# Two decode attentions in one kernel: PE's loop takes in the last chunk, and the fill products at a chunk's head get a count by chunk

## The chip, the cores and the metric

The kernel runs on one core of a Trainium2 chip. A core has a matrix engine (PE), a vector engine (DVE), a scalar engine (ACT), a general engine (POOL), a sync engine (SP) that here only issues transfers, and 16 DMA engines that move data between the device's memory (HBM) and the core's two memories, SBUF and, for PE's results, PSUM. The metric is the device time of one execution in microseconds (us). The span in a profile goes from the first to the last instruction; the time of the same execution is a little longer.

## The reference

Two attentions for one new token each, side by side, both with batch 4, 32 query heads of 128 and a cache of 8192 positions in bf16. A has 8 key heads, each shared by four query heads, and looks at the last W = 2048 positions; B has 32 key heads and looks at all.

```python
def _A_ref(x, k_cache, v_cache, wq, wo):
    q = (x @ wq).reshape(B, 1, 32, 128).transpose(0, 2, 1, 3)
    k = jnp.repeat(k_cache[:, :, Sk - W:, :], 4, axis=1)
    v = jnp.repeat(v_cache[:, :, Sk - W:, :], 4, axis=1)
    p = softmax(einsum("bhqd,bhkd->bhqk", q, k) * 128 ** -0.5)
    o = einsum("bhqk,bhkd->bhqd", p, v)
    return o.transpose(0, 2, 1, 3).reshape(B, 1, 4096) @ wo      # B x 1 x 512

# _B_ref: the same over the whole cache, with a key head for each query head
return jnp.concatenate([a, b], axis=-1)                         # 4 x 1 x 1024
```

Nearly all bytes are caches: 4 x 32 x 8192 x 128 x 2 bytes x 2 = 537 MB for B, and 34 MB for A.

## The kernel before

**Chunks.** A is cut into 8 chunks (a key head with the four batches), B into 32 (four heads of one batch): 256 tiles of 128 positions of K and as many of V, 8 MB each. Chunks of B are counted here from 0 to 31 (in the code `c - NCA`). Four chunks in a row share a piece of B's wo (512 KB).

**A chunk of B on PE** (`whole_B`, L910). First `reorder` (L820) multiplies the piece of wo, which lies in `wos`, into another order in four PSUM banks (three of `tr` and `po`); DVE takes these into `wol` (`take_wol`, L830). Between the two stand the fill products, `keep_busy(NBUSY)` (L905): products 128x512 of the identity into a bank of `sc`, which nobody reads. Then 32 groups of 8 transposes of K (`emit_T`, L541) into `tr`, whose results DVE and ACT copy to `kt`, and two groups later their scores (`emit_S`, L581, into `sc`). The first three groups of transposes need `wol`'s copies, since they take the same banks. The softmax is made in two halves (row maximum, the maximum over partitions, exp on ACT into `pbb`). Then 256 products with V (`emit_pv`, L733), the first 128 into `po`, the others into a bank of `tr`; then `norm_out` (DVE, into `oz`) and `emit_fin` (L835), eight products 4x256 of `oz` with `wol` that add to the bank `fin` over all 32 chunks. The stop flag of these products is set in the last products of the last chunk alone.

**Loops.** Every engine's program is written out as a list of operations with waits; `mark` (L90) cuts it at chunks. `_Sched.runs` (L123) looks for chunks whose operations read the same and whose waits differ by constant steps, and `emit_looped` (L164) writes such a run as a loop with its waits counted by a register; the rest is written out straight. The comparison holds what an operation says, its stop flag too; so PE's loop over B covers chunks 0 to 30, and chunk 31 is straight code behind it. An operation with `at` is given the register's value, by which it finds a place that moves from chunk to chunk.

**Transfers.** SP issues all large ones, in a fixed order on one queue: K of a chunk, V of it, K of the next. K of the next chunk waits until half of this chunk's K is transposed (L406, through POOL, which moves K's second half to a spare place, L421), V of the next until the products with V are through (L445). In the last chunks K and V come in pieces. Behind B's last V come the last two pieces of A's wo (L360); the products of A's last two chunks with them stand at the end of PE's program, and then the two halves of the output are copied by DVE (`emit_out`, L856) and stored.

Of the kernel before, what the change touches and what calls it, by code (L numbers as in the profile page):

```python
# [10 lines left out]
BF16 = mybir.dt.bfloat16  # L11
F32 = mybir.dt.float32

P = 128
# [18 lines left out]
QK = (0, 4, 8)  # L33
QC = (16, 24)
QV = (0, 8, 16, 24, 28)
NBUSY = 3

TRM0, BC0, L0, Q0, XT0 = 0, 256, 288, 320, 448
Z0 = Q0
# [18 lines left out]
class _Sched:  # L58
# [61 lines left out]
    def emit(self, engname, eng, sems):  # L120
        self.emit_ops(self.ops[engname], eng, sems)
# [55 lines left out]
def bass_concat_heads__sliding_block_cached__mha_block_cached__decode_kernel(  # L177
        nc, A_x, A_k, A_v, A_wq, A_wo, B_x, B_k, B_v, B_wq, B_wo, out):
    NB = A_x.shape[0]
# [4 lines left out]
    DO = A_wo.shape[1]  # L184
# [22 lines left out]
    NC = len(chunks)  # L207
    NCA = Hkv
# [13 lines left out]
    sch = _Sched()  # L222
    with ExitStack() as es:
        block = es.enter_context(nc.Block())

        def sb(name, shape, dt):
            return es.enter_context(nc.sbuf_tensor(name, shape, dt))

        def ps(name, shape, dt):
            return es.enter_context(nc.psum_tensor(name, shape, dt))  # L230
# [10 lines left out]
        identb = sb("identb", [P, P], BF16)  # L241
# [23 lines left out]
        pbt = {0: sb("pba", [P, NPB, NTA * 16 + NW], BF16), 1: sb("pbb", [P, 2, NTB * 2 + NW], BF16)}  # L265
        oT = sb("oT", [P, NSM, 16], BF16)
        oz = sb("oz", [P, 16], BF16)
        outsb = sb("outsb", [P, DO // 2], BF16)
        sel4 = sb("sel4", [P, 4, P], BF16)
        zA = sb("zA", [P, 2, 16], BF16)  # L270
# [4 lines left out]
        sc = ps("sc", [P, 2, 512], F32)  # L275
        po = ps("po", [P, 512], F32)
        ms = ps("ms", [P, 512], F32)
        fin = ps("fin", [P, 512], F32)
# [20 lines left out]
            out=ind[:, :].rearrange("u (x i) -> u x i", x=4), in_=onesf[0:4, :].rearrange("u (x i) -> u x i", x=4),  # L299
            pattern=[[1, 4], [0, P // 4]], compare_op=ALU.is_equal, fill=0.0, base=0, channel_multiplier=-1),  # L300
            waits=["c_onesf", "c_identf"], key="c_ind")
        sch.add("pool", lambda e: e.memset(oz[:, :], 0.0), waits=["c_ind"], key="c_oz")
        sch.add("pool", lambda e: e.memset(qb[:, :, :], 0.0), waits=["c_oz"])
        sch.add("pool", lambda e: e.memset(qq[:, :], 0.0), key="c_qb")

# [46 lines left out]
        def wo_slot(g):  # L352
            return g % 2
# [137 lines left out]
        def pe_mm(o, l, r, start=True, stop=True, transpose=False, waits=(), key=None):  # L491
            if transpose:
                sch.add("pe", lambda e: e.transpose(o, l, r), waits, key)  # L493
            else:
                sch.add("pe", lambda e: e.matmul(o, l, r, start=start, stop=stop), waits, key)  # L495
# [73 lines left out]
        def emit_qb(c, spare=False):  # L569

            if c >= NCA and not spare:
                col = NB * HQ + 4 * (c - NCA)
                sch.add("act", lambda e, x=0: e.activation(qq[:, 0:4], qs[:, bass.ds(x + col, 4)], ACTF.Copy), at=col,
                        waits=["c_qb"] + ([("S", chunks[c - 1]["s_last"])] if c > NCA else []), key=("qb", c))
                return
            waits = ["c_qb", ("q", 0)] if c < 2 else [("S", chunks[c - 2]["s_last"])]
            n, col = 16, 16 * c
            sch.add("dve", lambda e, x=0: e.tensor_copy(qb[:, c % 2, 0:n], qs[:, bass.ds(x + col, n)]), at=col,
                    waits=waits + ([("q", 1)] if c == 1 else []), key=("qb", c, "spare") if spare else ("qb", c))

        def emit_S(s):  # L581
            c, g = groups[s]
            ch = chunks[c]
            for t in range(TG):
                j = g * TG + t
                if ch["ab"] == 1:
                    bank, o0 = j // (NTB // 2), 4 * (j % (NTB // 2))
                else:
                    bank, o0 = j // HT, 16 * (j % HT)

                n = min(NW, 512 - o0)
                q = qb[:, c % 2, 0:n] if ch["ab"] == 0 else qq[:, 0:n]
                waits = []
                if t == 0:
                    waits = [("ev", s)] + sc_read[bank]
                    if g == 0:
                        waits += [("qb", c)]
                    sc_read[bank] = []
                pe_mm(sc[:, bank, o0:o0 + n], kt[:, s % NKT, t * P:(t + 1) * P], q,
                      waits=waits, key=("S", s) if t == TG - 1 else None)  # L600
# [184 lines left out]
        def add_first(c):  # L785

            pe_mm(po2[:, 0:4], identf[:, :], t1[:, :], start=False, stop=False, waits=[("t1", c)], key=("add", c))
            po_read[:] = [("t1", c)]
# [28 lines left out]
        def reord_at(u):  # L817
            return po[:, :] if u == 3 else tr[:, u, :].bitcast(F32)

        def reorder(c):  # L820

            for u in range(4):
                pp = slice(u * P // 4, (u + 1) * P // 4)
                for r in range(4):
                    pe_mm(reord_at(u), back[pp, r, :], wos[pp, r, :], start=r == 0, stop=r == 3,
                          waits=[("wr", c), ("c_back", 3)] if u == r == 0 else [],
                          key=("reord", c, u) if r == 3 else None)
            po_read[:] = [("wol", c, 3)]

        def take_wol(c):  # L830
            for u in range(4):
                o = reord_at(u)
                sch.add("dve", lambda e, u=u, o=o: e.tensor_copy(wol[:, u, :], o), waits=[("reord", c, u)], key=("wol", c, u))  # L833

        def emit_fin(c):  # L835
            ab = 0 if c < NCA else 1
            if ab == 1:
                ov = oz[:, :].rearrange("p (b u) -> p b u", b=NB)
                ops = [(ov[:, :, u], wol[:, u, :]) for u in range(4)]
                waits = ["c_oz", ("oT", c)]  # L840
            else:
                w = wor[:, wo_slot(c), :].rearrange("p (r n) -> p r n", r=4)
                ops = [(zA[:, c % 2, r * NB:(r + 1) * NB], w[:, r, :]) for r in range(4)]
                waits = [("z", c), ("wo", c)]
            lastc = NC - 1 if ab == 1 else NCA - 1

            for i, (l, r) in enumerate(ops):
                for h, (p0, x) in enumerate(out_halves(ab)):
                    pe_mm(fin[p0:p0 + NB, 0:DO // 2], l, r[:, x], start=False,
                          stop=i == len(ops) - 1 and c == lastc, waits=waits if i == h == 0 else [],  # L850
                          key=("fin", c) if i == len(ops) - 1 and h == 1 else None)

        def out_halves(ab):
            return [(64 * (1 - ab) + 32 * h, slice(h * DO // 2, (h + 1) * DO // 2)) for h in (0, 1)]

        def emit_out(c):  # L856
            ab = 0 if c < NCA else 1
            at = out_halves(ab)
            rows = slice(at[0][0], at[1][0] + NB)
            sch.add("dve", lambda e: e.tensor_copy(outsb[rows, :], fin[rows, 0:DO // 2]), waits=[("fin", c)], key=("osb", ab))  # L860
            for h, (p0, x) in enumerate(at):
                sch.add_dma("sp" if h else "act", lambda e, x=x, p0=p0: e.dma_start(out[:, 0, ab * DO + x.start:ab * DO + x.stop], outsb[p0:p0 + NB, :]),
                            "d_o%d" % h, waits=[("osb", ab)], key=("out", ab, h))
# [41 lines left out]
        def keep_busy(n):  # L905

            for _ in range(n):
                pe_mm(sc[:, 1, :], identb[:, :], sel4[:, :, :].rearrange("p r x -> p (r x)"))

        def whole_B(c):  # L910


            ch = chunks[c]
            sch.mark()
            reorder(c)
            keep_busy(NBUSY)
            take_wol(c)
            emit_qb(c)
            for g in range(ch["NG"]):
                emit_T(ch["s"] + g)  # L920
                if g >= SLAG:
                    emit_S(ch["s"] + g - SLAG)
                if g == 18:
                    stats_rowmax(c, 0)
                if g == 20:
                    stats_gmax(c, 0)
                if g == 22:
                    stats_bc(c, 0)
                if g == 23:
                    exp_B(c, 0, (0, 1))  # L930
                if g == 26:
                    exp_B(c, 0, (2, 3))
            for g in range(SLAG):
                emit_S(ch["s_last"] + 1 - SLAG + g)
            stats_rowmax(c, 1)
            for g in range(ch["NG"]):
                emit_pv(c, g)
                if g == 4:
                    stats_gmax(c, 1)
                if g == 8:  # L940
                    stats_bc(c, 1)
                    sums_B(c, 0)
                    exp_B(c, 1, (0, 1, 2, 3))
                    weigh_B(c)
                    sums_B(c, 1)
                    rest_sums(c)
                if g == 24:
                    norm_sum(c)
                if g == ch["NG"] - 2:
                    add_first(c)  # L950
            norm_out(c)
            emit_fin(c)

        def finish_A():
# [19 lines left out]
        for c in range(NCA, NC):  # L974
            whole_B(c)
        sch.mark()
        for c in range(NCA - LATEWO, NCA - 1):
            emit_fin(c)
        emit_out(NC - 1)
# [61 lines left out]
```

## Time and profile before

| | us |
|---|---|
| median of three runs | 1376.79 (1372.24 to 1378.86) |
| the profiled execution | 1376.78 |
| its span | 1375.0 |
| PE busy | 1200.1 |
| DVE, ACT, POOL busy | 770.3, 520.7, 234.5 |

In the profile's lists, L495 is the helper that records PE's products and L493 the one that records transposes, so groups are told apart by the tiles that they write and read (`tr<-identb,kv` is a transpose of K, `sc<-sel,identb` a fill product, `tr<-pbb,kv` and `po<-pbb,kv` the products with V). "<-POOLq L80" is a wait for the counter by which POOL passes on that K or V has landed. A number in brackets is the engine's idle time before the row and what ended it; "issue" means that nothing the profile shows was waited for. In rows of windows come the window, its length, busy time and instructions of PE, PE's weight loads, DVE, ACT and POOL, the granted clock of PE, the busy share of DMA and its GB/s.

### The profile page before, as it was taken

What the parts mean: (1) busy time and instruction counts of PE and PEld (TensorE: products, weight loads), DVE (VectorE), ACT (ScalarE), POOL (GpSimd) and SP (SyncE); (2) the same over time, 40 slices, a digit from 0 to 9 for tenths busy, and PEclk for the clock granted to TensorE, in tenths of its full rate; (3) what the DMA queues carried; (4) which work ended last, traced back from release to release, by engine and by line L of the source; (5) the groups of instructions that cost most, each with busy time, mean ns of one, the idle gap of its engine ahead of it and who ended that gap; (6) DMA issues with size and microseconds to landing.
All of it is one profiled execution on the core that took longest, in us unless ns stands there. A gap on an engine that the chain in (4) does not pass through costs nothing.

```text
span 1375.0 us, 62434 instructions
## 1 busy us (share of the span) xinstructions
PE 1200.1 (87%) x27697; PEld 1123.1 (82%) x27697; DVE 770.3 (56%) x1559; ACT 520.7 (38%) x713; POOL 234.5 (17%) x429
## 2 busy tenths in 40 slices
PE   4788788988888998989898998989899898999997
PEld 4787788878788988878788988878798788888887
DVE  1775455656455565645565565646556565555654
ACT  1553234333333443423343443323344342443443
POOL 2000002222220222222211222222112222000000
PEclk9998999999999999999999999999999999999999
DMA  9999999999999999999999999999999999999997
GB/s 401 423 428 429 427 443 427 431 429 429 438 435 435 433 431 431 431 431 433 438 427 435 435 425 433 415 450 418 429 431 429 440 423 427 437 427 425 428 427 330
DMA packets 18077, 587.64 MB, mean 427 GB/s; under 512 B 2024, under 2 KB 2048, under 8 KB 4096
## 3 DMA queue, kind: packets, MB, share of 16 engines
q1 hardware_dynamic: 18016, 587.21, 99.4%
q8 instruction: 21, 0.34, 0.1%
q14 instruction: 8, 0.07, 0.0%
q10 hardware_dynamic: 32, 0.01, 0.0%
HBM read 587.21 MB, written 0.01 MB: 427 GB/s over the span
## 4 chain that ended last, share of the span: by engine, by line
DMA 48%; PE 44%; issue 3%; DVE 3%; ACT 2%; ACTq 0%; SPq 0%; DVEq 0%; POOLq 0%
DMA kv<-in_B_k_cache_dram 43%; PE tr L493 24%; PE sc L495 11%; PE tr L495 4%; PE po L495 3%; DMA kv<-in_B_v_cache_dram 2%; DMA kv<-in_B_wq_dram 2%; PE ms L495 1%; DMA kv<-in_A_k_cache_dram 1%; DVE kt L564 1%; DVE wol L833 1%; ACT pba L716 1%; ACT pbb L686 1%; PE fin L495 1%; DVE sA L617 0%
## 5 line engine op out<-in xcount | busy, mean ns | idle before, releaser
L493 PE MATMUL tr<-identb,kv 128*128 128x128 bf16 x8704 | 683.2, 225 | 85.2 <-POOLq L80 73.9
L564 DVE COPY kt<-tr 128x1024 bf16<-128x1024 bf16 x736 | 503.2, 691 | 290.1 <-PE tr L493 287.1
L562 ACT ACTIVATE kt<-tr 128x1024 bf16<-128x1024 bf16 x352 | 359.7, 1024 | 698.9 <-PE tr L493 696.7
L493 PEld LDWEIGHTS tr<-identb,kv 128*128 128x128 bf16 x8704 | 529.2, 101 | 103.8 <-issue 69.9
L495 PE MATMUL sc<-qq,kt 128*128 128x64 bf16 x8192 | 403.5, 193 | 15.6 <-DVE kt L564 13.3
L421 POOL COPY kv<-kv 128x512 int32<-128x512 int32 x400 | 224.6, 616 | 923.1 <-DMA kv<-in_B_k_cache_dram 923.1
L495 PEld LDWEIGHTS sc<-qq,kt 128*128 128x128 bf16 x8192 | 333.6, 99 | 24.2 <-DVE kt L564 13.5
L686 ACT ACTIVATE pbb<-sc,negb 32x128 bf16<-32x128 f32 x256 | 138.0, 539 | 137.3 <-DVE negb L668 134.5
L495 PE MATMUL tr<-pbb,kv 128*128 128x64 bf16 x4096 | 135.6, 193 | 27.4 <-ACT pbb L686 25.5
L495 PEld LDWEIGHTS tr<-pbb,kv 128*128 128x128 bf16 x4096 | 130.9, 99 | 31.2 <-issue 30.3
L495 PE MATMUL po<-pbb,kv 128*128 128x64 bf16 x4096 | 135.1, 194 | 5.5 <-issue 4.4
L495 PEld LDWEIGHTS po<-pbb,kv 128*128 128x128 bf16 x4096 | 127.5, 98 | 5.3 <-issue 3.3
L833 DVE CAST wol<-tr 128x512 bf16<-128x512 f32 x96 | 60.4, 685 | 54.3 <-PE tr L495 52.6
L693 DVE TENSOR_REDUCE rs<-pbb 128x4 f32<-128x512 bf16 x32 | 22.0, 686 | 50.3 <-ACT pbb L686 50.3
L766 DVE RECIPROCAL ib<-ms 128x8 f32<-128x8 f32 x32 | 6.7, 208 | 57.7 <-PE ms L495 57.7
L495 PE MATMUL tr<-wos,back 32*128 32x512 bf16 x384 | 34.8, 383 | 0.4 <-issue 0.4
L495 PE MATMUL po<-wos,back 32*128 32x512 bf16 x128 | 33.9, 384 | 0.0
L654 DVE TENSOR_REDUCE gm<-ms 4x4 f32<-4x128 f32 x72 | 19.8, 275 | 20.8 <-PE ms L493 20.8
L634 DVE TENSOR_REDUCE rh<-sc 128x4 f32<-128x512 f32 x32 | 22.1, 692 | 14.3 <-PE sc L495 14.3
L668 DVE TENSOR_SCALAR negb<-ms 128x4 f32<-128x4 f32 x64 | 10.1, 157 | 32.0 <-PE ms L495 32.0
L495 PE MATMUL sc<-qb,kt 128*128 128x64 bf16 (+3 forms) x512 | 25.8, 195 | 2.1 <-issue 1.6
L495 PE MATMUL sc<-sel,identb 128*128 128x512 bf16 x96 | 26.9, 390 | 0.0
(82 smaller groups left out, 459.3 us busy)
## 6 DMA issues: line engine op xcount, KB each, us to landing
kv<-in_B_k_cache_dram SPq DMA_DIRECT2D x15, 2048.0 KB, 24.9
kv<-in_B_k_cache_dram SPq DMA_DIRECT2D x6, 4096.0 KB, 19.4
kv<-in_B_v_cache_dram SPq DMA_DIRECT2D x5, 4096.0 KB, 26.2
kv<-in_B_v_cache_dram SPq DMA_DIRECT2D x9, 2048.0 KB, 27.3
kv<-in_A_k_cache_dram SPq DMA_DIRECT2D x8, 2048.0 KB, 14.1
kv<-in_A_v_cache_dram SPq DMA_DIRECT2D x8, 2048.0 KB, 15.6
kv<-in_A_wq_dram SPq DMA_DIRECT2D x1, 4096.0 KB, 12.3
kv<-in_B_wq_dram SPq DMA_DIRECT2D x1, 4096.0 KB, 27.2
```

The costliest lines, as they stand in the source:

```text
L421: sch.add("pool", lambda e, dst=dst, org=org: e.tensor_copy(dst, org), waits=[("T", s0 + ch["NG"] - 1)] if g == 0 else [])
L493: sch.add("pe", lambda e: e.transpose(o, l, r), waits, key)
L495: sch.add("pe", lambda e: e.matmul(o, l, r, start=start, stop=stop), waits, key)
L562: sch.add("act", lambda e: e.activation(dst, src, ACTF.Copy), waits=waits, key=("ev", s))
L564: sch.add("dve", lambda e: e.tensor_copy(dst, src), waits=waits, key=("ev", s))
L634: sch.add("dve", lambda e: e.tensor_reduce(out=dst, in_=src, axis=AX.X, op=ALU.max), waits=[("S", ch["s"] + (half + 1) * ch["NG"] // 2 - 1 ...
L654: sch.add("dve", lambda e: e.tensor_reduce(out=gm[0:C, m, 0:U], in_=src, axis=AX.X, op=ALU.max), waits=[key_of("trm", c, half)], key=key_o ...
L668: sch.add("dve", lambda e: e.tensor_scalar(out=negb[:, m, 0:C], in0=ms[:, col:col + C], scalar1=-scale, scalar2=None, op0=ALU.mult), waits ...
L686: sch.add("act", lambda e, src=src, dst=dst, pp=pp, u=u: e.activation(dst, src, ACTF.Exp, bias=negb[pp, half, u:u + 1], scale=scale), wait ...
L693: sch.add("dve", lambda e: e.tensor_reduce(out=dst, in_=probs_of(c, half).rearrange("p j u -> p u j"), axis=AX.X, op=ALU.add), waits=[("ex ...
L716: sch.add("act", lambda e, b=b: e.activation(probs_of(c).rearrange("p j (b c) -> p j b c", b=NB)[:, :, b, :], eA[:, c % 2, :].rearrange("p ...
L833: sch.add("dve", lambda e, u=u, o=o: e.tensor_copy(wol[:, u, :], o), waits=[("reord", c, u)], key=("wol", c, u))
```

## The change

1. The stop flag of B's fin products is the same in all chunks (off). The sum is closed instead by two products with zeros behind the loop, one for each half of `fin`; DVE's copy of B's output waits for the second. A column block of zeros `zz` is made by POOL at the start for them.
2. With that, all 32 chunks of B say the same, and PE's loop covers them all; no chunk of B is left as straight code.
3. Two plain fill products stand at a head in place of three, and behind them a loop on PE over one more: it runs once in chunks 0 to 7 and 24 to 31, and eight times (1 + MOREBUSY) in chunks 8 to 23. Its count is worked out from the register of the loop over chunks.

```diff
-NBUSY = 3
+NBUSY = 2
+MOREBUSY = 7
...
+        zz = sb("zz", [P, NB], BF16)
...
-        sch.add("pool", lambda e: e.memset(oz[:, :], 0.0), waits=["c_ind"], key="c_oz")
+        sch.add("pool", lambda e: e.memset(oz[:, :], 0.0), waits=["c_ind"])
+        sch.add("pool", lambda e: e.memset(zz[:, :], 0.0), key="c_oz")
...
-            lastc = NC - 1 if ab == 1 else NCA - 1
...
-                          stop=i == len(ops) - 1 and c == lastc, waits=waits if i == h == 0 else [],
+                          stop=i == len(ops) - 1 and c == NCA - 1, waits=waits if i == h == 0 else [],
...
-            sch.add("dve", lambda e: e.tensor_copy(outsb[rows, :], fin[rows, 0:DO // 2]), waits=[("fin", c)], key=("osb", ab))
+            sch.add("dve", lambda e: e.tensor_copy(outsb[rows, :], fin[rows, 0:DO // 2]), waits=[("end", 32) if ab else ("fin", c)], key=("osb", ab))
...
+        def more_busy(c):
+            n = c - NCA
+            def mm(e):
+                return e.matmul(sc[:, 1, :], identb[:, :], sel4[:, :, :].rearrange("p r x -> p (r x)"), start=True, stop=True)
+            def emit(e, x=0):
+                if isinstance(e, _Record):
+                    return mm(e)
+                if isinstance(x, int):
+                    mm(e)
+                    return None
+                with nc.Fori(0, (((x + n + 8) >> 4) & 1) * MOREBUSY + 1, 1, engines=type(mybir.ALL_ENGINES)([mybir.EngineType.PE])):
+                    mm(e)
+                return None
+            sch.add("pe", emit, at=n)
...
             keep_busy(NBUSY)
+            more_busy(c)
             take_wol(c)
...
         sch.mark()
+        for p0, x in out_halves(1):
+            pe_mm(fin[p0:p0 + NB, 0:DO // 2], zz[:, :], sel4[:, 0:2, :].rearrange("p r x -> p (r x)"), start=False, key=("end", p0))
         for c in range(NCA - LATEWO, NCA - 1):
             emit_fin(c)
```

## The prediction

> **What bounds the kernel now.** The page comes first.
>
> ```profile
> span 1375.0 us, 62434 instructions
> PE 1200.1 (87%) x27697; PEld 1123.1 (82%) x27697; DVE 770.3 (56%) x1559; ACT 520.7 (38%) x713; POOL 234.5 (17%) x429
> q1 hardware_dynamic: 18016, 587.21, 99.4%
> q8 instruction: 21, 0.34, 0.1%
> ```
>
> One DMA queue is busy for 99.4% of the span. The kernel is bound by the transfer of 587 MB, and PE at 87% is the next resource, not the present one. Outside the span lie 1376.78 − 1375.0 = 1.8 us of the profiled execution, which stands at the median of the three runs (1376.79). So work taken from PE pays only where it lets DMA run closer to full, or after the last byte. Those two places have to be looked at: B's chunk heads and the tail.
>
> Heads: PE's timeline (start, duration, work, idle before), for two chunks and the head of a third, with SP's issues behind it.
>
> ```profile
> 547.69 1.33 PE L495 MATMUL po<-pbb,kv 128*128 128x64 bf16 x40
> 557.55 0.60 PE L495 MATMUL fin<-wol,oz 128*4 128x256 bf16 x8 [0.27 <-DVE oz L800]
> 558.17 0.41 PE L495 MATMUL tr<-wos,back 32*128 32x512 bf16 x3
> 559.18 0.82 PE L495 MATMUL sc<-sel,identb 128*128 128x512 bf16 x3
> 561.19 1.51 PE L493 MATMUL tr<-identb,kv 128*128 128x128 bf16 x24 [1.19 <-DVE wol L833]
> 595.49 0.82 PE L495 MATMUL sc<-sel,identb 128*128 128x512 bf16 x3
> 601.17 2.74 PE L493 MATMUL tr<-identb,kv 128*128 128x128 bf16 x24 [4.86 <-POOLq L80]
> 639.88 1.51 PE L493 MATMUL tr<-identb,kv 128*128 128x128 bf16 x24 [1.30 <-POOLq L80]
> ...
> 557.31 0.33 SPq L445 DMA_DIRECT2D kv<-in_B_v_cache_dram  x1
> 593.65 0.33 SPq L445 DMA_DIRECT2D kv<-in_B_v_cache_dram  x1
> 635.92 0.33 SPq L445 DMA_DIRECT2D kv<-in_B_v_cache_dram  x1
> ```
>
> Chunks alternate. One whose K was waited for 4.86 us runs its first 24 transposes in 2.74 us; the next, after 1.30 us, takes 1.51. The windows give the clock behind that (third number from the end): 0.50 at another cold head, 1.00 at the warm one.
>
> ```profile
> 522.48:525.98 3.50, 3.50 (x38) 3.50 (x39) 1.38 (x2) 0.72 (x1) 3.50 (x7) 0.50 0.82 356
> 561.19:563.50 2.31, 2.31 (x45) 2.17 (x46) 1.81 (x3) 0.76 (x1) 2.31 (x5) 1.00 1.05 454
> ```
>
> From T's start to the issue of the next V a warm chunk needs 593.65 − 561.19 = 32.5 us, a cold one 635.92 − 601.17 = 34.8. So a cold chunk puts V into the queue only 639.88 − 635.92 = 4.0 us before the K ahead of it has landed; after a warm one the lead was 601.17 − 593.65 = 7.5. Now the windows from one landing of K to the next.
>
> ```profile
> 483.76:522.46 38.70, 33.74 (x805) 31.58 (x805) 22.03 (x43) 14.75 (x20) 8.98 (x16) 0.98 1.00 434
> 561.18:601.15 39.97, 33.73 (x805) 31.58 (x805) 22.57 (x44) 14.74 (x20) 8.98 (x16) 0.98 1.00 433
> 639.86:679.33 39.47, 33.73 (x805) 31.58 (x805) 22.46 (x44) 14.75 (x20) 8.98 (x16) 0.98 0.99 429
> 718.04:758.31 40.27, 34.00 (x808) 31.86 (x809) 22.61 (x44) 14.76 (x20) 8.99 (x16) 0.98 0.99 430
> 758.31:796.73 38.42, 35.82 (x805) 33.80 (x802) 21.65 (x43) 14.77 (x20) 8.98 (x17) 0.93 1.02 437
> 796.73:836.46 39.73, 33.73 (x805) 31.59 (x805) 22.53 (x44) 14.76 (x20) 8.98 (x17) 0.98 1.00 432
> 875.16:915.61 40.45, 33.73 (x805) 31.58 (x805) 22.58 (x44) 14.76 (x20) 8.99 (x16) 0.97 1.01 436
> 954.32:994.00 39.68, 33.73 (x805) 31.59 (x805) 22.26 (x44) 14.75 (x20) 8.98 (x17) 0.98 1.01 436
> ```
>
> The first number of a row is the spacing, the last the rate in GB/s. The base is 38.70 us, or 39.97 where a piece of wo (every fourth chunk) rides along. Against it the later six rows lose 0.77, 0.30, −0.28, 1.03, 0.48 and 0.98 us, 3.3 us together, and each loss follows a V issued late by a cold chunk. I read them as queues that ran dry for a moment at the short lead, though the share of 0.99 to 1.01 is too coarse to show it.
>
> The tail: what PE waits for in the last chunk, the last of the transfers and the close.
>
> ```profile
> 1348.68 0.34 PE L495 MATMUL sc<-qq,kt 128*128 128x64 bf16 x6 [1.19 <-issue]
> 1355.43 0.22 PE L493 MATMUL tr<-identb,kv 128*128 128x128 bf16 x1 [0.74 <-issue]
> 1361.90 0.19 PE L495 MATMUL po<-pbb,kv 128*128 128x64 bf16 x1 [1.24 <-issue]
> 1368.11 1.22 PE L495 MATMUL tr<-pbb,kv 128*128 128x64 bf16 x36 [0.94 <-issue]
> ...
> 1369.00:1369.50 0.50, 0.50 (x18) 0.50 (x15) 0.00 (x0) 0.00 (x0) 0.00 (x0) 1.00 0.24 82
> 1369.50:1370.00 0.50, 0.50 (x23) 0.50 (x21) 0.37 (x2) 0.00 (x0) 0.00 (x0) 1.00 0.00 0
> ...
> 1371.67 1.09 PE fin L495 x24
> 1372.78 0.43 DVE outsb L860
> ```
>
> Four stalls that wait for nothing shown, 6 to 7 us apart, stand in the last chunk, which PE runs as straight code behind its loop. The instruction queue moved 21 packets of 0.34/21 MB = 16 KB in all: the loop is not fetched anew in each round, and the stalls fit one fetch for each 16 KB of the straight code. They add up to 4.1 us. The chain runs along PE here, but the last data arrive only at 1369.5.
>
> **The change, part by part.**
>
> *Last chunk in the loop.* It removes the 4.1 us. Fin would start at 1371.67 − 4.1 = 1367.6. The last bytes are A's two wo pieces; with the last fin products needing them at 1369.5, plus 0.6 for a group (the row of 8 at 557.55), PE ends at 1370.1 and the last copy starts there instead of at 1372.78: 2.7 us gained. Bounds: 4.1 if the transfers end earlier too, 0 if the loop's exit now waits for its code. The code behind the loop is some 50 instructions, so one such fetch would cost one stall of the four, about 1.2.
>
> *The two closing products* on zeros, 128x256 as fin's: 24 of those took 1.09 us, so 0.1 for two, ahead of wo's landing and covered by it. Uncovered, 0.1. The extra memset on POOL delays the constants behind it by 0.1 (oz's row); PE's first big products wait for wq's landing meanwhile, which covers it.
>
> ```profile
> L302 POOL MEMSET oz<- 128x16 bf16 x1 | 0.1, 113 | 0.1
> L495 PE MATMUL ms<-xT,kv 128*128 128x4 bf16 x256 | 7.1, 166 | 8.3 <-DMA kv<-in_A_wq_dram 4.4 <-DMA kv<-in_B_wq_dram 3.9
> L495 PE MATMUL sc<-sel,identb 128*128 128x512 bf16 x96 | 26.9, 390 | 0.0
> ```
>
> *Fill at a head, one round* (16 outer chunks). Two plain fills and one in a loop stand for three. New are register work for the count and a branch not taken; no row has their price. From below 0; from above, the big loop's own way back: between fin's start at 557.55 and 558.17 PE's queue issued 8 pairs (33 ns each by the row of 40 in 1.33 us, 0.27) and the branch, so 0.35 at most. I take 0.2. In the last chunks, where PE is on the chain, this lies under DVE's first kt copy of the chunk, which comes behind its wol copies:
>
> ```profile
> 1261.24 1.81 PE L493 MATMUL tr<-identb,kv 128*128 128x128 bf16 x24
> 1263.71 0.41 PE L495 MATMUL sc<-qq,kt 128*128 128x64 bf16 x8 [0.65 <-DVE kt L564]
> ```
>
> PE waits 0.65 for kt there, which covers it; without that cover three heads would cost 0.6, and the 1.4 between the stalls' 4.1 and the 2.7 taken would still swallow it.
>
> *Eight rounds* (chunks 8 to 23). A round costs p: at least the 0.215 us between two fills ((0.82 − 0.39)/2, with 0.39 the mean of one in the last row above), at most 0.35 + 0.03 = 0.38 by the bound above. I take 0.3, between. In a warm chunk fills begin 595.49 − 561.19 = 34.3 us after K landed; two plain ones 0.4, the count 0.2, eight rounds 2.4: they end at 37.3 (36.4 to 38.1 by the bounds). K lands at 38.70 or 39.97, so PE still waits 1.4 us, or 2.7 where wo came along. Hence nothing is delayed: what queues behind the fills (T of the next chunk, and behind it K's and V's issues on SP) waits for K anyway.
>
> *What the shorter wait changes.* Is 2.7 us short enough to stay warm? The nearest rows:
>
> ```profile
> 405.09 2.74 PE L493 MATMUL tr<-identb,kv 128*128 128x128 bf16 x24 [2.11 <-POOLq L80]
> 483.77 1.51 PE L493 MATMUL tr<-identb,kv 128*128 128x128 bf16 x24 [2.11 <-POOLq L80]
> ```
>
> The same wait of 2.11 us once ended cold and once warm. So the ordinary chunks should be warm, those behind wo pieces in about half the cases. A warm chunk issues V 2.3 us sooner, at a lead of 38.70 − 32.5 = 6.2, where no landing was late. Of the 3.3 us lost I count 2.0 as won back (bounds 0 and 3.3). The Trainium skill (TensorE: Matmul & The Clock Gate, "HAM oscillation — how this bites in real kernels") asks only that PE has no gaps over about 3.4 us; by it every wait here would stay warm and all 3.3 would come back, but the row at 405.09 is cold after 2.11, and I side with the row.
>
> **Sum:** 1376.78 − 2.7 − 2.0 = 1372.1 us.
>
> **Rivals.**
>
> *All of it comes back.* Every head stays warm (3.3) and the transfers that end earlier by this let the whole 4.1 count: 1376.8 − 7.4 = 1369.4. For it: no late landing at a lead of 6 or more. Against it: the losses may be the memory's own, as 0.28 was gained once.
>
> *Little is moved.* The losses are not the clock's, and the loop's exit takes one fetch: 2.7 − 1.2 = 1.5, so 1375.3. For it: DMA at 99.4% and rows whose lead is as short (557.31, 3.9 us ahead of 561.18) without a loss behind them.
>
> *Slower: the rounds hold PE up.* A small loop's way back is dearer than the big one's, whose branch may have been hidden behind fin's work. It decides when 34.3 + 0.4 + 0.2 + 8p passes the mean spacing of K, (3 × 38.70 + 39.97)/4 = 39.0: from p = 0.51 on, PE is the bound in 16 chunks. At p = 0.7 each loses 40.5 − 39.0 = 1.5, together 24, less the tail's 2.7: 1398. Against it: the bound of 0.38; for it: no row has a loop of two instructions. The Trainium skill (Advanced Engine Details and Errata, "Control Flow Timing") gives a compare-and-branch some 108 ns; an estimate from it, one after the other with the product's 0.215, is p = 0.32, which leaves the sum as it is.
>
> **How the numbers follow.** Forecast 0.48, all of it 0.22, little 0.17, slower 0.13. The three runs of before lie from 1372.24 to 1378.86, about 0.5%, and less than that can't be told from no change: 6.9 us, so faster begins at 1369.9. Of the second case three quarters fall under that and of the forecast a sixth (0.165 + 0.08): faster 0.25; slower 0.14, the last case and a hundredth of noise; same 0.61. The forecast's own range is 1369 to 1376; with both unknown terms and the noise, and most of the slower case left out, 1367 to 1381.
>
> **What would show it.** Right: the instruction queue loses about seven packets; no stall of that kind in the last chunk; 208 fills in place of 96, (2 + 1) × 32 + 7 × 16; in chunks 8 to 23 waits for K of 1 to 3 us and first transposes near 1.5; landings of K at 38.70 and 39.97 throughout; fin's end set by wo. Wrong: waits for K gone and spacings above 40 us from chunk 8 to 23 (rounds too dear), first transposes still at 2.74 after short waits (the clock does not follow the fills), or warm heads with losses in K's spacing as before (they were the memory's).

## The result and the profile after

| | before | after |
|---|---|---|
| median us | 1376.11 (20 runs, 1372.24 to 1379.57) | 1371.15 (20 runs, 1369.62 to 1373.35) |
| ratio | 1 | 0.9967, interval 0.9958 to 0.9977 |
| span of the profiled execution | 1375.0 | 1369.8 |
| chunk 26's K landed, from the span's start | 1150.28 | 1148.07 |
| from there to the end | 224.7 | 221.7 |

The change takes off 5.0 us by the medians, 0.36% (0.33% by the ratio). The interval leaves out 1, so the kernel is faster, but by less than the 0.5% that I had set as telling. The two last rows split the profiled 5.2 us into 2.2 in the middle and 3.0 in the tail.

In the lists of the changed kernel the two helpers stand at L498 and L496, the counted fill at L917 and POOL's counter at L81. Its page, the instruction queue and the fills:

```profile
span 1369.8 us, 63325 instructions
q1 hardware_dynamic: 18016, 587.21, 99.7%
q8 instruction: 15, 0.25, 0.1%
...
L917 PE MATMUL sc<-sel,identb 128*128 128x512 bf16 x144 | 47.4, 384 | 13.5 <-issue 13.5
```

Six packets of code less, where about seven were forecast. The 144 fills of the counted loop, with the 64 plain ones, make the 208 that were to be. Each of the 144 is as long as a plain one (384 ns), but 13.5 us of idle time stand before them. One head in PE's timeline shows where:

```profile
482.03 0.60 PE L498 MATMUL sc<-sel,identb 128*128 128x512 bf16 x2
482.47 1.03 PE L917 MATMUL sc<-sel,identb 128*128 128x512 bf16 x4
483.67 0.39 PE L917 MATMUL sc<-sel,identb 128*128 128x512 bf16 x1 [0.17 <-issue]
484.27 0.39 PE L917 MATMUL sc<-sel,identb 128*128 128x512 bf16 x1 [0.21 <-issue]
484.88 0.39 PE L917 MATMUL sc<-sel,identb 128*128 128x512 bf16 x1 [0.22 <-issue]
485.50 0.39 PE L917 MATMUL sc<-sel,identb 128*128 128x512 bf16 x1 [0.23 <-issue]
486.17 1.51 PE L496 MATMUL tr<-identb,kv 128*128 128x128 bf16 x24 [0.27 <-issue]
```

Four rounds come at the pace of plain fills (3 × 0.215 + 0.39 = 1.03), the later ones 0.61 us apart with PE idle between them, for nothing the profile shows. So the transposes begin at 486.17, though K had landed at 483.79.

The heads and the spacing of K's landings, from the windows:

```profile
445.10:483.79 38.69, 37.11 (x809) 34.72 (x809) 21.37 (x42) 14.76 (x20) 8.97 (x17) 0.92 1.00 434
483.79:523.38 39.59, 36.67 (x815) 32.43 (x814) 22.80 (x45) 14.74 (x20) 8.97 (x16) 1.00 0.99 427
523.38:562.07 38.69, 36.16 (x813) 32.28 (x813) 22.03 (x43) 14.76 (x20) 8.97 (x16) 1.00 1.00 430
562.07:602.05 39.98, 36.44 (x814) 32.35 (x813) 22.02 (x43) 14.74 (x20) 8.97 (x16) 1.00 1.01 434
640.75:679.45 38.70, 35.94 (x812) 32.25 (x812) 22.03 (x43) 14.74 (x20) 8.98 (x17) 1.00 1.00 434
991.62:1030.69 39.07, 36.32 (x814) 32.35 (x813) 22.03 (x43) 14.74 (x20) 8.97 (x16) 1.00 1.01 435
```

Of the 16 spacings from chunk 8 on, two stand off 38.70 and 39.97: 39.59, behind chunk 8, whose head was cold (2.74 us for its first transposes) and at whose end V was issued only 3.6 us ahead of K's landing, and 39.07. The losses have become 1.3 us where they were 3.5. SP's rows give the lead in a warm stretch:

```profile
518.62 0.33 SPq L448 DMA_DIRECT2D kv<-in_B_v_cache_dram  x1
557.06 0.33 SPq L448 DMA_DIRECT2D kv<-in_B_v_cache_dram  x1
```

523.38 − 518.62 = 4.8 and 562.07 − 557.06 = 5.0 us, less than the 6.2 that I forecast, because the fills end after K's landing.

The tail, PE's timeline:

```profile
1364.41 0.87 PE L498 MATMUL tr<-pbb,kv 128*128 128x64 bf16 x24 [0.54 <-POOLq L81]
1365.12 0.36 PE L498 MATMUL tr<-t,identf 128*128 128x4 f32 x2
1365.34 0.39 PE L498 MATMUL tr<-pbb,kv 128*128 128x64 bf16 x8
1366.01 0.60 PE L498 MATMUL fin<-wol,oz 128*4 128x256 bf16 x8 [0.27 <-DVE oz L803]
1366.38 0.27 PE L498 MATMUL fin<-wor,zA 128*4 128x256 bf16 x2
1366.44 0.28 PE L498 MATMUL fin<-sel,zz 128*4 128x256 bf16 x2
1366.49 0.97 PE L498 MATMUL fin<-wor,zA 128*4 128x256 bf16 x14
```

None of the four stalls is left. One wait of 0.54 us has come in their place, for V's last piece; behind it everything runs on, the products with A's wo among it.

### The profile page after: what moved, and what is told of

Read it like the earlier page. It is cut to its first block, busy times and chain, and to the rows that moved or that the text cites. A ratio compares the mean times of both kernels' runs of the same rounds, so it can differ in the third digit from the quotient of the medians.

```text
span 1369.8 us, 63325 instructions
## 1 busy us (share of the span) xinstructions
PE 1227.1 (90%) x27811; PEld 1125.7 (82%) x27811; DVE 769.4 (56%) x1559; ACT 520.5 (38%) x713; POOL 234.2 (17%) x430
## 3 DMA queue, kind: packets, MB, share of 16 engines
q1 hardware_dynamic: 18016, 587.21, 99.7%
## 4 chain that ended last, share of the span: by engine, by line
PE 52%; DMA 37%; issue 4%; DVE 3%; ACT 2%; ACTq 0%; SPq 0%; DVEq 0%; POOLq 0%
DMA kv<-in_B_k_cache_dram 31%; PE tr L496 26%; PE sc L498 13%; PE tr L498 6%; DMA kv<-in_B_v_cache_dram 5%; PE po L498 4%; DMA kv<-in_B_wq_dram 2%; PE sc L917 2%; PE ms L498 2%; DVE kt L567 1%; ACT pbb L689 1%; ACT pba L719 1%; DVE sA L620 1%; PE fin L498 1%; DVE wol L836 0%
## 5 line engine op out<-in xcount | busy, mean ns | idle before, releaser
L496 PE MATMUL tr<-identb,kv 128*128 128x128 bf16 x8704 | 675.1, 223 | 40.9 <-POOLq L81 36.1
L496 PEld LDWEIGHTS tr<-identb,kv 128*128 128x128 bf16 x8704 | 521.6, 100 | 57.5 <-issue 41.0
L498 PE MATMUL sc<-qq,kt 128*128 128x64 bf16 x8192 | 400.4, 192 | 15.4 <-DVE kt L567 14.0
L498 PEld LDWEIGHTS sc<-qq,kt 128*128 128x128 bf16 x8192 | 330.0, 98 | 23.4 <-DVE kt L567 12.7
L498 PE MATMUL tr<-pbb,kv 128*128 128x64 bf16 x4096 | 136.5, 193 | 26.1 <-ACT pbb L689 25.6
L498 PEld LDWEIGHTS tr<-pbb,kv 128*128 128x128 bf16 x4096 | 131.9, 100 | 29.8 <-issue 29.2
L498 PE MATMUL po<-pbb,kv 128*128 128x64 bf16 x4096 | 135.1, 194 | 4.5 <-issue 3.2
L498 PEld LDWEIGHTS po<-pbb,kv 128*128 128x128 bf16 x4096 | 127.5, 98 | 5.6 <-issue 3.3
L917 PE MATMUL sc<-sel,identb 128*128 128x512 bf16 x144 | 47.4, 384 | 13.5 <-issue 13.5
L917 PEld LDWEIGHTS sc<-sel,identb 128*128 128x128 bf16 x144 | 13.9, 97 | 45.0 <-issue 37.4
L498 PE MATMUL tr<-wos,back 32*128 32x512 bf16 x384 | 34.0, 375 | 0.5 <-issue 0.5
L498 PE MATMUL po<-wos,back 32*128 32x512 bf16 x128 | 33.0, 377 | 0.0
L657 DVE TENSOR_REDUCE gm<-ms 4x4 f32<-4x128 f32 x72 | 19.8, 274 | 17.5 <-PE ms L496 17.5
```

The lines of the kernel that those rows point to most:

```text
L657: sch.add("dve", lambda e: e.tensor_reduce(out=gm[0:C, m, 0:U], in_=src, axis=AX.X, op=ALU.max), waits=[key_of("trm", c, half)], key=key_o ...
L917: return e.matmul(sc[:, 1, :], identb[:, :], sel4[:, :, :].rearrange("p r x -> p (r x)"), start=True, stop=True)
```

## Experiments

Times are medians of 4 to 12 executions; ratios are against runs of the kernel before on the same chip. The runs were made on four chips, on which the median of the kernel before lay between 1375.4 and 1376.9, so that much stands between times of different chips.

| run | us | ratio, interval |
|---|---|---|
| e1_loop: loop over 32 chunks alone | 1373.96 | 0.9984, 0.9970 to 0.9997 |
| e2_fill: counted fills alone | 1374.09 | 0.9984, 0.9972 to 0.9995 |
| e3_halves: before, V in halves | 1373.06 | 0.9983, 0.9971 to 0.9994 |
| e4_late: before, V issued later | 1381.03 | 1.0042, 1.0025 to 1.0059 |
| e5_rounds10: after, ten rounds | 1388.64 | 1.0093, 1.0060 to 1.0126 |
| e6_loop_halves: e1 with V in halves | 1371.64 | 0.9965, 0.9952 to 0.9978 |
| e7_after_halves: after, V in halves | 1371.69 | 0.9967, 0.9953 to 0.9980 |
| e8_plain10: e1 with ten plain fills | 1371.85 | 0.9964, 0.9947 to 0.9981 |
| e9_after_late: after, V issued later | 1377.24 | 0.9996, 0.9983 to 1.0009 |
| e10_after_tail: after, V in halves in chunks 27 and 28 | 1371.07 | 0.9963, 0.9948 to 0.9978 |
| e11_rounds5_tail: e10 with five rounds | 1370.79 | 0.9951, 0.9937 to 0.9966 |
| e12_ends_halves: e11, halves in chunks 1 to 8 too | 1370.42 | 0.9961, 0.9949 to 0.9974 |

### The two parts alone

The loop, against after:

```diff
-NBUSY = 2
-MOREBUSY = 7
+NBUSY = 3
...
-            more_busy(c)
```

> Only the stop flags and the closing products: PE's loop covers all 32 chunks, three plain fills as before. My theory (two separate gains): the four stalls of the last chunk are gone, K's landings lose as much between chunks 8 and 24 as before, so about 1376.1 - 2.9 = 1373.2 us; K's landing of chunk 26 stays near 1150. Rival (the gain is the fills' alone, the last chunk waits for data anyway): 1375.5 to 1376.5. Rival (the loop is all): 1371 to 1372.

The fills, against after (the closing products are left out too):

```diff
-                          stop=i == len(ops) - 1 and c == NCA - 1, ...
+                          stop=i == len(ops) - 1 and c == (NC - 1 if ab == 1 else NCA - 1), ...
```

> Only the fills by a counted loop; the last chunk stays straight code behind PE's loop over 31. My theory: K's landing of chunk 26 about 2.2 us earlier than before (1148 for 1150), the four stalls of about 1 us stay, so about 1376.1 - 2.2 = 1373.9 us. Rival (the fills do nothing, the landings scatter by themselves): 1376. Rival (the fills are all): 1371 to 1372.

The loop alone gives 2.5 us, the fills alone 2.3, both together 5.0. By the intervals each part alone may be anything from 0.4 to 4.1 us, so the times by themselves don't show that the two add; the places in the traces show that they are separate. With the loop alone, chunk 26's K lands at 1150.66, as late as before, and no stall is left in the last chunk. With the fills alone it lands at 1147.89, and the last chunk keeps its stalls; PE's timeline of that run:

```profile
1346.73 0.41 PE L498 MATMUL sc<-qq,kt 128*128 128x64 bf16 x8 [0.65 <-issue]
1352.94 0.34 PE L496 MATMUL tr<-identb,kv 128*128 128x128 bf16 x3 [0.24 <-issue]
1359.15 0.26 PE L498 MATMUL po<-pbb,kv 128*128 128x64 bf16 x3 [0.90 <-issue]
1365.35 1.30 PE L498 MATMUL tr<-pbb,kv 128*128 128x64 bf16 x39 [0.96 <-issue]
```

They are again 6.2 us apart, and that run's instruction queue shows the 21 packets of before. Straight code and stalls go together, and the loop takes both away. The times of the single packets in the traces tie them closer. In the kernel before none lies between 166.7 and 1339.5 us, so the loop's rounds fetched nothing, and six lie behind that. The four stalls end 1.3 to 1.5 us after the end of one of these (1347.19 and 1348.68, 1354.12 and 1355.43, 1360.48 and 1361.90, 1366.65 and 1368.11); with the fills alone it is 1.4 to 1.5 us each time. In the changed kernel the last packet lies at 165.6, so the loop's exit fetched nothing either.

### Is it V's lead in the queue?

V in halves, against before:

```diff
-            return QUARTERS if c == NCA else HALVES if c == NCA + 1 else LASTV if c == NC - 1 else NEXTV if c >= NC - 3 else WHOLE
+            return QUARTERS if c == NCA else LASTV if c == NC - 1 else NEXTV if c >= NC - 3 else HALVES
```

> The kernel before, but V comes in two halves in all the chunks where it came whole, so that its first half is issued when the first 128 products with V are through, some 5 us sooner. No fill is added and the heads stay as cold as before. If short leads of V in the queue are what costs (my theory), K's landings stand at 38.70 and 39.97 throughout and the time falls by 2 to 3.3, to 1373 to 1374 us. Rival (the clock itself, through PE's time, costs): no change, 1376. Rival (the memory's own scatter): no change, 1376. Rival (more pieces cost something on the queue): above 1377.

V later, against before:

```diff
-waits = ... else [("pv", c - 1, 0 if j0 + n <= NTB // 2 else 1)]
+waits = ... else [("fin", c - 1)] if len(pieces) == 1 else [("pv", c - 1, 0 if j0 + n <= NTB // 2 else 1)]
```

> The kernel before, but whole V waits for the fin products of the chunk ahead instead of its last product with V, so it is issued about 0.9 us later. If the queue runs dry at a short lead (my theory), every V behind a cold chunk now comes 3.1 us instead of 4.0 ahead of K's landing, and some 12 landings lose 0.5 to 0.9 us more: 1381 to 1387 us. Rival (the memory's own scatter): no change, 1376.

Both moved as the lead says and against the other readings. POOL's copies begin when K has landed; its timeline in the run with halves (start, duration, work, idle before):

```profile
640.93 8.96 POOL L421 COPY kv<-kv 128x512 int32<-128x512 int32 x16 [29.82 <-DMA kv<-in_B_k_cache_dram]
679.71 8.96 POOL L421 COPY kv<-kv 128x512 int32<-128x512 int32 x16 [29.82 <-DMA kv<-in_B_k_cache_dram]
718.50 8.96 POOL L421 COPY kv<-kv 128x512 int32<-128x512 int32 x16 [29.83 <-DMA kv<-in_B_k_cache_dram]
758.57 8.95 POOL L421 COPY kv<-kv 128x512 int32<-128x512 int32 x16 [31.11 <-DMA kv<-in_B_k_cache_dram]
797.34 8.96 POOL L421 COPY kv<-kv 128x512 int32<-128x512 int32 x16 [29.82 <-DMA kv<-in_B_k_cache_dram]
836.13 8.95 POOL L421 COPY kv<-kv 128x512 int32<-128x512 int32 x16 [29.83 <-DMA kv<-in_B_k_cache_dram]
```

Every spacing is 38.8 or 40.1, though from chunk 13 on every other head is as cold in this run as before (2.74 us for the first transposes at 679.73, as at 601.17 before). Its times lie within 2.1 us of each other (1372.76 to 1374.89), where those of before spread over 7.3. The scatter of the landings, and most of that of the runs, went with the short leads. The price is 0.08 us for each chunk (38.78 for 38.70), 2.0 in the 24 spacings: more pieces do cost something, but less than they save.

With V later, the same view and SP's issues:

```profile
719.41 8.96 POOL L421 COPY kv<-kv 128x512 int32<-128x512 int32 x16 [29.76 <-DMA kv<-in_B_k_cache_dram]
761.23 8.95 POOL L421 COPY kv<-kv 128x512 int32<-128x512 int32 x16 [32.85 <-DMA kv<-in_B_k_cache_dram]
799.63 8.96 POOL L421 COPY kv<-kv 128x512 int32<-128x512 int32 x16 [29.45 <-DMA kv<-in_B_k_cache_dram]
840.82 8.96 POOL L421 COPY kv<-kv 128x512 int32<-128x512 int32 x16 [32.23 <-DMA kv<-in_B_k_cache_dram]
...
796.86 0.33 SPq L445 DMA_DIRECT2D kv<-in_B_v_cache_dram  x1
```

The V issued at 796.86 has a lead of 799.63 − 796.86 = 2.8 us, and the next K lands 41.19 us after the one before it, 2.5 over the base. The whole run is 4.6 us slower, at the lower edge of what was expected: most landings lost less than 0.5, a few lost far more.

The packets in the traces tell what runs dry. A transfer's packets of 64 KB go to 16 engines, and these end K one after another: in this run between 796.43 and 799.01 us. V, issued at 796.86, has its first packet at 797.81, so the first that was through stood still for at least 1.4 us. In the kernel before, at the landing of 639.86, the engines end K between 637.45 and 639.24; a V issued at 635.92, 4.0 us ahead of the landing by POOL's copies, is only 1.5 us ahead of the first engine that runs out, and V's first packets took up to 3.5 us there for the usual 2.4.

The same delay on the changed kernel:

> The changed kernel with whole V issued behind the fin products, 0.9 us later, as was done to the kernel before. My theory (the fills bought lead, and lead is what counts): the leads of 4.8 to 6.2 us in the middle shrink to 3.9 to 5.3, so some loss comes back there, and in the outer chunks the cold heads lose as the kernel before did with late V: 1373 to 1376 us. Rival (what the fills bought doesn't hang on the lead): 1371.2 to 1372.

It took 1377.24: the whole gain is gone, more than expected. The profiled execution, 2.5 us above this median, has lost 9.4 us in K's spacings up to chunk 26, for 1.3 in the changed kernel, about half of it in the chunks with eight rounds. From chunk 26's K to the end it takes 1378.0 − 1156.35 = 221.7 as there, so what the loop saves in the tail is still there.

### Do the fills act by anything but the lead?

The loop with V in halves, and with the counted fills on top:

> The loop over all 32 chunks, three plain fills, and V in halves wherever it came whole. If the two gains are separate and add: 1373.1 - 2.9 = 1370.2 us, with K's landings even at 38.78 and 40.06. If the earlier V only moves the wait to the tail: 1371.5 to 1373.

> The changed kernel (loop and counted fills) with V in halves. My theory (the fills act only through V's lead in the queue): nothing is left for them, so the same as the loop with halves and three fills, 1370.2 us within 0.5. Rival (a warm clock gives something of its own): 1 to 2 us below the loop with halves. Rival (the dearer rounds cost something that the short leads hid): 1 to 2 us above it.

1371.64 and 1371.69 (all 24 runs between 1371.42 and 1371.82): where V comes early in any case, the fills give nothing, and their slow rounds cost nothing. So in this kernel the fills are seen to act through V's lead alone. The sum of the parts, 1370.2, was missed by 1.4, and what held was the other case, that the earlier V moves a wait to the tail. The reason is in the halves' own run: there the time from chunk 26's K to the end had already fallen to 1371.3 − 1148.9 = 222.4 from 224.7, so a part of its gain was the tail's, and the loop could take only another 1.4 there (221.0).

### What does a round cost?

Two rounds more, against after:

```diff
-MOREBUSY = 7
+MOREBUSY = 9
```

> The changed kernel with MOREBUSY 9, ten rounds in chunks 8 to 23 in place of eight. In the changed kernel's trace the first four rounds take 0.215 us each and the later ones 0.61, and chunks that don't wait for K follow each other at 38.44 us on PE, against 39.02 for K. My theory (each further round is paid on PE at 0.61): 38.44 + 1.21 = 39.65, PE becomes the bound, 16 x 0.63 = 10 us later, with 1 to 3 us taken up by the wait that is there at chunk 8: 1378 to 1381 us. Rival (further rounds go under the wait for K): 1371, as with eight.

PE becomes the bound, as the theory has it, but the loss against the changed kernel is 17.5 us where 7 to 10 were expected. PE's timeline, heads of following chunks:

```profile
524.52 1.51 PE L496 MATMUL tr<-identb,kv 128*128 128x128 bf16 x24 [0.31 <-issue]
564.20 1.51 PE L496 MATMUL tr<-identb,kv 128*128 128x128 bf16 x24 [0.27 <-issue]
603.93 2.74 PE L496 MATMUL tr<-identb,kv 128*128 128x128 bf16 x24 [0.27 <-issue]
```

and two windows, the rounds ahead of the third head and its first transposes:

```profile
600.20:603.90 3.70, 2.29 (x6) 0.53 (x6) 0.85 (x2) 0.00 (x0) 2.76 (x5) 0.99 0.94 407
603.93:607.40 3.47, 3.47 (x38) 3.47 (x39) 1.38 (x2) 0.69 (x1) 3.47 (x8) 0.52 1.00 434
```

564.20 − 524.52 = 39.68 us is the pace that 0.61 to the round gives. But at 603.93 PE is cold, 0.27 us after its last fill: the clock fell to 0.52 although no gap before it was over 0.3 us. This happened at six of the sixteen heads, and a chunk behind such a head took 41.0 to 41.2 us. In the profiled execution fifteen times 0.66 and five times 1.4 make 17, and the last of the sixteen chunks, whose next head has one round again, gives 2.5 back: 14.5, for a span that is 14.8 longer than the changed kernel's (the medians differ by more, 17.5). So slow rounds are poor fill: at the pace of plain fills PE would need 0.215 of each 0.61, about a third (the profile counts each product's whole 0.39 as busy, 2.29 of 3.70 in the window).

Ten plain fills at every head, against e1: `NBUSY = 10`.

> The loop over all 32 chunks, and ten plain fills at every head, no counted loop. My theory: plain fills keep the pace of 0.215 us, so the seven more end 1.5 us later and leave a wait for K of 2 to 3.3 us; heads are warm in about half the chunks, the middle gains 1 to 2 us; the last chunks, bound by PE, lose up to 0.85 us each in three or four heads, of which the wait for the last data hides 1.4: 1372 to 1375 us. Rival (only the rounds' length counts, not the clock): the middle gains nothing, 1374 to 1376.

1371.85, level with the changed kernel, better than expected. The plain fills leave PE waiting 0.6 to 3.4 us for K, the heads vary (1.5 to 2.7 us), and yet the leads are 4.8 to 7.5 and K's spacings lose only 0.8 in all. The last chunks do pay: they take 36.45 us for 36.08. The counted loop is thus not needed for the gain; it spares the last chunks the fill, and pays for that with slow rounds in the middle.

### Better versions

> The changed kernel with V in halves in chunks 27 and 28 alone, where K already comes in halves and PE has caught up with DMA. With halves everywhere the time from chunk 26's K to the end was 221.0 us, with whole V 221.7; if that is those two chunks' V, the time is 0.5 to 0.7 lower: 1370.5 to 1370.7 us. Rival (the end hangs on the last bytes, which come no sooner): 1371.2.

> As the run before, with MOREBUSY 4: five rounds in chunks 8 to 23, of which only the last is a dear one. The fills end 1.8 us sooner, PE waits 1 to 2 us for K and has 38.44 - 1.8 = 36.6 us to a chunk, so V's lead rises by up to 1.8 us where the head stays warm. If lead counts: as good or better than eight rounds, 1369.8 to 1370.7 us. Rival (the shorter fill leaves more cold heads, whose V is late again): 1371 to 1373.

> As the run before (loop, five rounds in chunks 8 to 23, V in halves in chunks 27 and 28), with V in halves in chunks 1 to 8 as well, where the heads are cold without the long fill and K's landings lost 1 to 4 us in the last traces. If lead counts: the landings there stand at 38.78 and 40.06, 0.08 for each chunk is paid, and the runs gather near the lowest ones of the run before: 1369.5 to 1370.5 us. Rival (the losses of those chunks are the memory's): 1371.

The edits are `HALVES if c >= NC - 5` in place of `WHOLE`, then `MOREBUSY = 4`, then halves for chunks 1 to 8 as well. 1371.07, 1370.79 and 1370.42: all are ahead of the kernel before, but their intervals overlap with the changed kernel's, so none is shown to beat it. In the first, the time from chunk 26's K to the end is 1371.1 − 1150.15 = 221.0, shorter by the 0.7 expected, while chunks 2 to 8, which have no long fill, lost more in that execution. The last run put the halves there: spacings of 38.75 to 38.80 (40.05 to 40.08 where wo rides along) without a loss, and five of its six runs between 1370.35 and 1370.54. That evenness is its clearest gain.

## Why the prediction was right

**The bound** held: DMA went from 99.4% to 99.7%, and only what touched the queue's feeding or the tail moved the time, up to the ten rounds that made PE the bound.

**The tail**, forecast at 2.7, measured 3.0 in the profiles and 2.5 by the loop alone. The size was right by a reason half wrong. I set fin's end by the landing of A's wo; no product waited for it. What PE waits for last is V's last piece, with 0.54 us. Counted from chunk 26's K, fin starts 3.5 us sooner (1366.01 − 1148.07 = 217.94 for 1371.67 − 1150.28 = 221.39), which is the stalls' 4.1 less 0.54 and a tenth. Then 0.4 is lost: from fin's start to the last copy of the output (at 1367.51) it takes 1.5 us, for 1.1 before, as B's eight products now run ahead of A's sixteen and no longer between them. So about 3.0 is left, and that this lies near 2.7 is luck: the terms behind it are others. The reading of the stalls as fetches of straight code stood, by the packets' times.

**The middle**, forecast at 2.0, measured 2.2 and 2.3 by the fills alone. That short leads make K late was argued before and is now shown, by moving the lead in both directions (later without any other change, sooner by a split). It is not so each time: leads of 3.5 to 4.3 us lost between nothing and 1.9. Nor is each loss a lead's. In the changed kernel the 39.07 follows a lead of 4.9, with DMA at its full rate from K to V; it dips at 995, where the trace has an 8 KB packet on the other instruction queue, q14. Two spacings of the later runs, with five rounds or V in halves at the end, lost 0.55 behind leads of 6.2, each with such a packet in it. Most of these packets cost nothing, and no run moved them. And before with V later lost 0.64 behind a lead of 6.6 with neither a gap nor such a packet: in the middle of V DMA moved 410 to 418 GB/s for ten us, where 434 is usual. So a part of the losses is not the lead's, and its cause stays open. My "no landing was late" at 6.2 does not hold in every run.

**The price of a round** was the term mis-sized: 0.3, at most 0.38, against 0.215 for the first four and 0.61 for the others, 0.46 on the mean ((486.17 − 482.47)/8). The bound came from the big loop's way back, and the rival's remark on it fits: there the branch may have been hidden behind products already in PE's queue, as the small loop's first rounds go at the plain pace. Hence the fills did not end under the wait for K, as "nothing is delayed" had it, but up to 2.4 us behind its landing (486.17 for 483.79), and the sign "waits for K of 1 to 3 us" failed at most heads. Chunks then follow at 38.44 us on PE against the 39.0 of K; the mean of 0.46 lies just under the 0.51 from which I let the slower case decide, and two rounds more crossed that line.

**The clock**: "ordinary chunks should be warm, those behind wo pieces in about half the cases" came near by count, but not for the reason given. Of the twelve ordinary heads eleven were warm, of the four where wo rode along one. But the waits were not the 1.4 and 2.7 us of the sum: most heads had none, and cold or partly cold ones came at 445, 679, 758 and 914 us, after waits of 0.5 to 1.8 us, and after 0.3 with ten rounds. Two of them:

```profile
679.46 2.58 PE L496 MATMUL tr<-identb,kv 128*128 128x128 bf16 x24 [0.54 <-POOLq L81]
758.15 2.74 PE L496 MATMUL tr<-identb,kv 128*128 128x128 bf16 x24 [0.56 <-POOLq L81]
```

The rule of the Trainium skill (TensorE: Matmul & The Clock Gate, "HAM oscillation — how this bites in real kernels"), no gaps over about 3.4 us, would have had them all warm; the rows stand against it as the one at 405.09 did. The traces' clock records add one thing: in the runs before, after, with the loop alone, V in halves, ten rounds and ten plain fills the granted clock changes only at points that lie whole steps of 3.41 us apart. With ten rounds the cold heads come in pairs (603.93 and 645.08, 805.20 and 846.41, 1006.55 and 1047.72), and the pairs follow each other after 201.3 us, 59 such steps. So the place of a sparse stretch between these points seems to count, which would let one wait of 2.11 us end cold and another warm; no run was made to test it. That the full 3.3 did not come back is due for 0.9 us to the cold head at 445 and its lead of 3.6; the other 0.4 is the spacing of 39.07.

**The rivals**: "all of it comes back" missed by what the paragraphs on the tail and the clock name. "Little is moved" fell with the two single parts. The slower one was near: 0.46 for the 0.51 from which it would have decided.

## What to carry to other kernels

When one DMA queue is full on the average, look at how long before the last landing the next large transfer is issued: here leads of about 4 us lost between nothing and 1.9 us, leads under 3 us, with V issued later, 1.1 to 2.5, and leads of about 9 and more nothing. The landing of the whole transfer is a late mark for this, since the first of its 16 engines is through up to 2.6 us before the last. Splitting a transfer so that its first half can go earlier bought the same as warming PE, without a product. Fill for a clock must be dense: a loop of one product was not, from its fifth round on. And a last iteration left as straight code by a flag can cost its fetches where nothing follows to hide them.

## What the runs showed of the hardware

- A round of one product 128x512 in a loop with a register's count takes 0.61 us on PE's queue, with the product itself at a pace of 0.215; the first four went at the pace of plain ones.
- The granted clock fell to about a half while PE had no gap over 0.3 us, with rounds of 0.61 us around products of a pace of 0.215 (six of sixteen heads with ten rounds).
- Straight code of 16 KB pieces stalled PE 0.2 to 1.2 us at most pieces under a full DMA queue, at 6 to 7 us of work to the piece; each stall ended 1.3 to 1.5 us after the end of a packet on the instruction queue. The loop, which had seven such packets in its first round, was not fetched again in 32 rounds.
- One more piece in the transfer of 8 MB cost 0.08 us.
- The 16 engines ended a transfer of 8 MB 1.8 to 2.6 us apart (1.8 in the kernel before at the landing of 639.86, 2.6 with V issued later), and the next transfer's first packet came 0.95 us after its issue (796.86 and 797.81, V issued later).
